# Keys mixed two rows at a time, and batch 0's plan of interleaved stages reordered

## Chip, cores and metric

One core of a Trainium2 chip. The metric is the device time of the whole kernel in microseconds (us). All runs quoted are fast; those of the kernel before run from 374.6 to 377.5 us over all sessions, so versions are compared by ratios within the same rounds. A ratio here is the mean time of one kernel's fast runs over that of the other's of the same rounds, so it is not quite the ratio of the medians that are quoted beside it.

## The reference

Attention within blocks whose keys and values are first mixed across blocks by a normalized 8x8 matrix `P` per head, then a mixture of four two-layer experts. Cut to what matters (`P` comes from five rounds of exponential and normalization of `sort_net`):

```python
B, H, S, D = 4, 8, 768, 64            # 8 blocks of 96 rows
k_sorted = einsum('bhij,bhjcd->bhicd', P, k_b)
v_sorted = einsum('bhij,bhjcd->bhicd', P, v_b)
attn = softmax(scale * q_b @ k_sorted.T)          # block by block
x = (attn @ v_sorted) as [3072, 512]
out = sum over e of p[:, e] * (relu(x @ w1[e]) @ w2[e])   # w1 [4,512,1024]
```

## The kernel before

TensorE runs the experts of batch b in three chunks of 256 rows; the attention of batch b+1 is cut into small stages which a plan puts into slots between groups of expert matmuls. `(1, 5, st_s, 1)` means: chunk 1, slot 5, scores of the second pair of heads. In batch 0 a chunk has slots 0 to 5 behind the groups of the first layer (16 matmuls each) and 6 to 12 behind the products of the second.

```python
    def load_queries(b, heads=range(H)):           # one load per head, on GpSimd
        ...
            nc.gpsimd.dma_start(t[:, h // 2, :, h % 2, :], q[b, h].rearrange("(t p) d -> p t d", p=P))

    def st_q(b, pr):                               # queries of a pair, transposed by a DMA from SP
        qT = att.tile([P, R, P], F16, name=f"qT_{b}_{pr}", tag="qT", bufs=3)
        nc.sync.dma_start_transpose(
            qT[:], natural[(b, "q")][:, pr].rearrange("p t h d -> p (t h d)")
        )
        ...

    def st_k(b, pr):                               # keys of a pair, mixed and transposed
        ps = psa([P, R, P], F32, f"ps_k_{b}_{pr}")
        for r in range(R):
            for hh in range(2):
                h = 2 * pr + hh
                nc.tensor.matmul(
                    ps[ds(D * hh, D), r, :],
                    head(b, "k", h)[:, r, :],
                    PIk[(b * H + h) // 4][:, h % 4, :, :].rearrange("p i c -> p (i c)"),
                    start=True, stop=True,
                )
        kT = kTs[pr % 2]
        nc.scalar.copy(
            kT[:, 0:S].rearrange("p (i r c) -> p i r c", i=NB, r=R),
            ps.rearrange("p r (i c) -> p i r c", c=CP),
        )

    def st_s(b, pr):                               # scores: 16 matmuls that read kT and qT
        kT, qT = kTs[pr % 2], qTs[(b, pr)]
        pss = [psa([P, 2, 512], F32, f"ps_s_{b}_{pr}_{hh}") for hh in range(2)]
        ...

    # st_n loads a pair's queries; st_lv, st_lk, st_lq load the next batch's values, keys, queries
    PLAN0 = [
        (0, 9, st_v, 0), (0, 10, st_q, 0), (0, 10, st_v, 1), (0, 11, st_k, 0), (0, 11, st_n, 1), (1, 0, st_q, 1),
        (1, 0, st_s, 0), (1, 0, st_n, 2), (1, 1, st_k, 1), (1, 1, st_v, 2), (1, 2, st_v, 3), (1, 3, st_a, 0),
        (1, 4, st_x, 0), (1, 3, st_q, 2), (1, 4, st_n, 3), (1, 5, st_s, 1), (1, 6, st_k, 2), (1, 8, st_a, 1),
        (1, 7, st_lv, 0), (1, 9, st_x, 1), (1, 10, st_s, 2), (1, 9, st_lv, 1), (1, 9, st_q, 3), (1, 11, st_k, 3),
        (1, 12, st_a, 2), (1, 12, st_lk, 0),
        (2, 0, st_lq, 0), (2, 1, st_x, 2), (2, 2, st_lk, 1), (2, 2, st_s, 3), (2, 8, st_a, 3), (2, 9, st_x, 3),
    ]

    def chunk(b, c, slot, done=()):                # [...] parts of batch 0's second layer
        def f1():
            nc.scalar.copy(p1[:], product("p1", blk(0, 0), "b11"))
            slot()
            gtt(oa1, oa1, p1[:], ALU.add)          # gtt: GpSimd, tt: VectorE
        ...
        def store(n, tile):
            nc.sync.dma_start(o[:, 2 * c + n, :], tile[:])
        ...
            next(sums0)                            # a weight difference on VectorE
            tt(u2[:], product("p6", sm(1), "t2"), p1[:], ALU.add)
            slot()
```

`psa` and `psm` are pools of two PSUM buffers each: `psa` for the stages, `psm` for the experts.

The softmax here doesn't subtract the row's maximum and nothing guards it: scores larger than these inputs give would overflow.

Of the kernel before, what the change touches and what calls it, by code (L numbers as in the profile page):

```python
# [9 lines left out]
F32 = mybir.dt.float32  # L10
# [7 lines left out]
def kernel(  # L18
# [11 lines left out]
    nc = tc.nc  # L30

    B, H, S, D = q.shape
# [33 lines left out]
    def psa(shape, dtype, name):  # L66
        state["n"] += 1
        return psA.tile(shape, dtype, tag="ps", name=name)
# [47 lines left out]
    def head(b, nm, h):  # L116
        return natural[(b, nm, h // 4)][:, h % 4, :, :]
# [117 lines left out]
    qTs = {}  # L235

    def warm(n):
        ps = psA.tile([P, 4, P], F32, tag="ps", name=f"ps_w_{state['n']}")
        state["n"] += 1
        for m in range(n):  # L240
            nc.tensor.matmul(ps[:, m % 4, :], dummy, dummy, start=True, stop=True)  # L241
# [21 lines left out]
    nc.gpsimd.tensor_copy(ident6, ident[0:R, 0:R])  # L263
    for it in range(5):
        nc.scalar.activation(sn[:], sn[:], AF.Exp, bias=0.0, scale=1.0)
        if it >= 3:
            h_q(it - 3, 0, nc.scalar.copy)
            warm(20 - 8 * (it - 3))
        nc.vector.tensor_reduce(srow[:], sn[:], AX.X, ALU.add)
        nc.vector.reciprocal(srow[:], srow[:])  # L270
        nc.vector.tensor_tensor(sn[:], sn[:], srow[:].broadcast_to([GH, NB, NB]), ALU.mult)
        nc.vector.tensor_reduce(scol[:], sn[:].rearrange("p i j -> p j i"), AX.X, ALU.add)
        nc.vector.reciprocal(scol[:], scol[:])
        if it < 4:
            nc.vector.tensor_tensor(
                sn[:], sn[:],
                scol[:].rearrange("p j o -> p o j").broadcast_to([GH, NB, NB]),
                ALU.mult,
            )
            if it:  # L280
                next(p_steps)
# [87 lines left out]
        qTs[(b, pr)] = qT.rearrange("p t x -> p (t x)").rearrange("p (i x) -> p i x", i=NB)  # L369

    def st_k(b, pr):
        ps = psa([P, R, P], F32, f"ps_k_{b}_{pr}")
        for r in range(R):
            for hh in range(2):
                h = 2 * pr + hh
                nc.tensor.matmul(  # L376
                    ps[ds(D * hh, D), r, :],
                    head(b, "k", h)[:, r, :],
                    PIk[(b * H + h) // 4][:, h % 4, :, :].rearrange("p i c -> p (i c)"),
                    start=True, stop=True,  # L380
                )
        kT = kTs[pr % 2]
        nc.scalar.copy(  # L383
            kT[:, 0:S].rearrange("p (i r c) -> p i r c", i=NB, r=R),
            ps.rearrange("p r (i c) -> p i r c", c=CP),
        )

    def st_s(b, pr):
        kT, qT = kTs[pr % 2], qTs[(b, pr)]
# [190 lines left out]
    def stage(b, f, pr):  # L580
# [18 lines left out]

    PLAN0 = [  # L600
        (0, 9, st_v, 0), (0, 10, st_q, 0), (0, 10, st_v, 1), (0, 11, st_k, 0), (0, 11, st_n, 1), (1, 0, st_q, 1),
        (1, 0, st_s, 0), (1, 0, st_n, 2), (1, 1, st_k, 1), (1, 1, st_v, 2), (1, 2, st_v, 3), (1, 3, st_a, 0),
        (1, 4, st_x, 0), (1, 3, st_q, 2), (1, 4, st_n, 3), (1, 5, st_s, 1), (1, 6, st_k, 2), (1, 8, st_a, 1),
        (1, 7, st_lv, 0), (1, 9, st_x, 1), (1, 10, st_s, 2), (1, 9, st_lv, 1), (1, 9, st_q, 3), (1, 11, st_k, 3),
        (1, 12, st_a, 2), (1, 12, st_lk, 0),
        (2, 0, st_lq, 0), (2, 1, st_x, 2), (2, 2, st_lk, 1), (2, 2, st_s, 3), (2, 8, st_a, 3), (2, 9, st_x, 3),
    ]


# [135 lines left out]
    def chunk(b, c, slot, done=()):  # L745

        es = range(E) if b else range(1, E)
        todo = [e for e in es if e not in done]
        chunk_first(b, c, todo, todo[0], slot)
        for w in range(1, 4 if b or c else 3):  # L750
            h_sums(E - 1, w)
        if (b, c) != (B - 1, R // 2 - 1):
            nxt = (b, c + 1) if c + 1 < R // 2 else (b + 1, 0)
            pbs[nxt] = load_p(*nxt)

        blk = lambda kh, tok: (lambda e, f: Hb[:, e, kh * KH + f, ds(tok * P, P)])
        sm = lambda n: (lambda e, f: Sb[:, n, e, ds(f * P, P)])

        def product(n, lhs, rhs):
            ps = psm([P, DH], F32, f"ps_{n}_{b}_{c}")  # L760
            for e in es:
                for f in range(KH):
                    nc.tensor.matmul(  # L763
                        ps[:], lhs(e, f), Ts[e][rhs][:, f, :],
                        start=(e == es[0] and f == 0), stop=(e == E - 1 and f == KH - 1),
                    )
            return ps[:]

        if b:
            oa, ob = [moeo.tile([P, Dm], F32, name=f"{n}_{b}_{c}", tag="oacc") for n in ("oa", "ob")]  # L770
        else:
            oa, ob = oaccs[2 * c], oaccs[2 * c + 1]
        p1, p5, u2, u3 = [moe.tile([P, DH], F32, name=f"{n}_{b}_{c}", tag=n, bufs=1) for n in ("p1", "p5", "u2", "u3")]
        tt, gtt = nc.vector.tensor_tensor, nc.gpsimd.tensor_tensor
        o = out[ds(b * S, S), :].rearrange("(t p) d -> p t d", p=P)
        oa1, oa2, ob1, ob2 = oa[:, 0:DH], oa[:, DH:Dm], ob[:, 0:DH], ob[:, DH:Dm]
        if b:
            nc.scalar.copy(p1[:], product("p1", blk(0, 0), "b11"))  # L778
            slot()
            nc.scalar.copy(ob1, product("p4", blk(1, 1), "n4"))  # L780
            slot()
            tt(oa1, product("p2", blk(1, 0), "b21"), p1[:], ALU.add)
            slot()
            nc.scalar.copy(p5[:], product("p5", sm(0), "t1"))
            slot()
            for e in es:
                h_sums(e, 4)
            tt(u2[:], product("p6", sm(1), "t2"), p1[:], ALU.add)  # L788
            slot()
            gtt(oa2, u2[:], p5[:], ALU.add)  # L790
            tt(u3[:], product("p7", sm(2), "t3"), u2[:], ALU.add)
            slot()
            gtt(ob2, u3[:], p5[:], ALU.add)
            tt(ob1, ob1, u3[:], ALU.add)
            nc.sync.dma_start(o[:, 2 * c + 1, :], ob[:])
            tt(oa2, product("p3", sm(3), "b22"), oa2, ALU.add)
            slot()
            nc.sync.dma_start(o[:, 2 * c, :], oa[:])
            return
        def f1():  # L800
            nc.scalar.copy(p1[:], product("p1", blk(0, 0), "b11"))
            slot()
            gtt(oa1, oa1, p1[:], ALU.add)

        def f2():
            tt(oa1, product("p2", blk(1, 0), "b21"), oa1, ALU.add)
            slot()

        def f3():
            tt(oa2, product("p3", sm(3), "b22"), oa2, ALU.add)  # L810
            slot()

        def f4():
            tt(ob1, product("p4", blk(1, 1), "n4"), ob1, ALU.add)
            slot()

        def f5():
            nc.scalar.copy(p5[:], product("p5", sm(0), "t1"))
            slot()
            gtt(oa2, oa2, p5[:], ALU.add)  # L820
            gtt(ob2, ob2, p5[:], ALU.add)

        def last(u3):
            gtt(ob2, u3, ob2, ALU.add)
            tt(ob1, ob1, u3, ALU.add)

        def store(n, tile):
            nc.sync.dma_start(o[:, 2 * c + n, :], tile[:])

        if c == 0:  # L830

            steps = weight_sums(E - 1, nc.vector)
            f1()
            for e in todo:
                h_sums(e, 4)
            next(steps)
            f2()
            next(steps)
            h_sums(E - 1, 3)
            f3()  # L840
            next(steps)
            f5()
            next(steps)
            tt(u3[:], product("p7", sm(2), "t3"), p1[:], ALU.add)
            slot()
            ps6 = product("p6", sm(1), "t2")
            tt(u2[:], ps6, p1[:], ALU.add)
            tt(u3[:], ps6, u3[:], ALU.add)
            slot()
            gtt(oa2, u2[:], oa2, ALU.add)  # L850
            store(0, oa)
            last(u3[:])
            f4()
            store(1, ob)
        else:
            f1()
            f4()
            f2()
            f5()
            for e in todo:  # L860
                h_sums(e, 4)
            next(sums0)
            tt(u2[:], product("p6", sm(1), "t2"), p1[:], ALU.add)  # L863
            slot()
            gtt(oa2, u2[:], oa2, ALU.add)
            next(sums0)
            tt(u3[:], product("p7", sm(2), "t3"), u2[:], ALU.add)
            slot()
            last(u3[:])
            store(1, ob)  # L870
            f3()
            store(0, oa)
# [75 lines left out]
    for qd in range(2):  # L948
# [8 lines left out]
        [(h_v, 1, 1, act)],  # L957
        [(h_s, 0, 2)],
        [(h_w, 0, vec), (h_s, 1, 2)],
        [(h_w, 1, vec), (h_a, 0, 2)],  # L960
        [(h_s, 0, 3), (h_a, 1, 2)],
        [(h_s, 1, 3), (h_a, 0, 3)],
        [(h_x, 2, act), (h_a, 1, 3)],
# [65 lines left out]
```

## Time and profile before

| | before |
|---|---|
| time | 375.25 us (374.92 to 375.5), over all sessions 374.62 to 377.49 |
| span in the profile | 373.0 us |
| TensorE, VectorE, ScalarE, GpSimd busy | 98%, 70%, 20%, 24% |
| granted TensorE clock | 0.999 |

The prediction below shows the lines on what bounds it.

`natq` are the queries as loaded and `qT` their transposes. The weights, on the same GpSimd queue (POOLq) as the queries, need 27 us to land (median): they are issued faster than they land, and the last of them, issued at about 22 us, lands at about 60.

### The profile page before, as it was taken

The numbers are of one execution on the slowest core, as the hardware profiler recorded it, in microseconds if no ns is written. First come the engines' busy times: TensorE is split into PE (matmuls) and PEld (weight loads), VectorE is DVE, ScalarE is ACT, GpSimd is POOL, SyncE is SP. The second block draws the span as 40 slices with busy tenths as digits, with TensorE's granted clock in tenths as the row PEclk, the third lists the DMA queues.
The fourth block names the chain that finished last, engine by engine and source line by source line (L and its number), as shares of the span: only waits on it lengthen the run. The fifth ranks groups of instructions, "written<-read, shape, count | busy, mean of one in ns | idle before, by whom it ended". The sixth has DMA issues, their size and how long they took to land.

```text
span 373.0 us, 9188 instructions
## 1 busy us (share of the span) xinstructions
PE 366.3 (98%) x4013; PEld 314.9 (84%) x4013; DVE 261.2 (70%) x470; ACT 73.9 (20%) x120; POOL 87.9 (24%) x122
## 2 busy tenths in 40 slices
PE   8999999999999999999999999999999999999996
PEld 8785858888888888888898888888889888888885
DVE  5654798679888774795694684696695693774872
ACT  2673330423210233012100224012101000000000
POOL 8772101804577203002911000000000001001001
PEclk9999999999999999999999999999999999999999
DMA  7999999999995658642962322505203101121001
GB/s 104 207 207 229 208 209 197 190 163 143 187 154 137 110 77 133 126 80 43 124 71 48 101 66 60 138 2 77 79 2 79 57 15 44 56 47 50 19 3 56
DMA packets 69603, 38.25 MB, mean 103 GB/s; under 512 B 40374, under 2 KB 64444, under 8 KB 69564
## 3 DMA queue, kind: packets, MB, share of 16 engines
q0 software_dynamic: 34640, 17.83, 37.6%
q1 hardware_dynamic: 34924, 19.85, 26.0%
q8 instruction: 31, 0.51, 0.6%
q14 instruction: 8, 0.07, 0.1%
HBM read 42.00 MB, written 6.34 MB: 130 GB/s over the span
## 4 chain that ended last, share of the span: by engine, by line
PE 87%; DMA 8%; DVE 2%; POOL 1%; issue 1%; ACT 0%; DVEq 0%
PE ps_h L730 40%; PE ps_p L763 35%; DMA w<-in_moe_w_dram 4%; PE ps_o L670 3%; DMA qT<-natq 2%; PE ps_w L241 2%; DMA natq<-in_q_dram 2%; PE ps_h L635 1%; PE ps_s L393 1%; PE ps_a L425 1%; PE ps_k L376 1%; PE ps_v L345 1%; POOL sn L284 0%; DVE xsl L410 0%; POOL T L136 0%
## 5 line engine op out<-in xcount | busy, mean ns | idle before, releaser
L730 PE MATMUL ps_h<-xT,w 128*128 128x256 f16 x1440 | 163.0, 273 | 0.0
L730 PEld LDWEIGHTS <-w 128*128 128x128 f16 x1440 | 139.5, 98 | 17.8
L736 DVE SCALAR_TENSOR_TENSOR Hb<-ps_h,pb 128x1024 f16<-128x1024 f32 x90 | 110.1, 1224 | 40.1 <-PE ps_h L730 38.3
L763 PEld LDWEIGHTS <-Sb 128*128 128x128 f16 x720 | 69.5, 98 | 9.6 <-issue 0.5
L763 PEld LDWEIGHTS <-Hb 128*128 128x128 f16 x540 | 52.1, 98 | 6.8 <-issue 0.4
L790 POOL TENSOR_TENSOR oa<-u,p 128x256 f32<-128x256 f32 x9 | 6.5, 723 | 176.7 <-issue 161.9
L763 PE MATMUL ps_p<-w,Sb 128*128 128x256 f16 x360 | 43.2, 273 | 0.3 <-DVE u L863 0.3
L763 PE MATMUL ps_p<-w,Hb 128*128 128x256 f16 x360 | 43.2, 273 | 0.0
L763 PE MATMUL ps_p<-T,Sb 128*128 128x256 f16 x360 | 42.3, 273 | 0.0
L400 ACT ACTIVATE ET<-ps_s 96x768 f16<-96x768 f32 x24 | 18.1, 802 | 54.4 <-PE ps_s L393 54.4
L114 POOL DMA_DIRECT2D natq<-in_q_dram x24 | 19.9, 851 | 14.3 <-DMA w<-in_moe_w_dram 10.2
L778 ACT COPY p<-ps_p 128x256 f32<-128x256 f32 x9 | 3.4, 373 | 93.3 <-PE ps_p L763 50.1
L763 PE MATMUL ps_p<-T,Hb 128*128 128x256 f16 x180 | 21.6, 273 | 0.0
L715 DVE TENSOR_TENSOR Sb<-Sb,Hb 128x512 f16<-128x512 f16 x45 | 19.6, 436 | 0.4
L717 DVE TENSOR_TENSOR Sb<-Hb 128x512 f16<-128x512 f16 x45 | 18.8, 418 | 0.0
L713 DVE TENSOR_TENSOR Sb<-Hb 128x512 f16<-128x512 f16 x45 | 18.8, 417 | 0.0
L410 DVE TENSOR_TENSOR xsl<-ps_a,rz 96x512 f16<-96x512 f32 x24 | 16.5, 686 | 0.8
L719 DVE TENSOR_TENSOR Sb<-Hb,Sb 128x512 f16<-128x512 f16 x45 | 16.6, 427 | 0.0
L383 ACT CAST kT<-ps_k 128x768 f16<-128x768 f32 x12 | 9.6, 799 | 35.4 <-PE ps_k L376 35.3
L788 DVE TENSOR_TENSOR u<-ps_p,p 128x256 f32<-128x256 f32 x9 | 3.8, 426 | 17.9 <-PE ps_p L763 17.9
L351 ACT CAST vo<-ps_v 128x768 f16<-128x768 f32 x12 | 9.5, 801 | 21.5 <-PE ps_v L345 19.8
L103 POOL DMA_DIRECT2D nat_k<-in_k_dram x8 | 6.1, 767 | 31.9 <-PE ps_k L376 27.8
(131 smaller groups left out, 300.9 us busy)
## 6 DMA issues: line engine op xcount, KB each, us to landing
w<-in_moe_w_dram POOLq DMA_DIRECT2D x7, 1024.0 KB, 27.1
pb<-p_dram SPq DMA_DIRECT2D x12, 512.0 KB, 5.1
nat_k<-in_k_dram POOLq DMA_DIRECT2D x8, 384.0 KB, 7.4
nat_v<-in_v_dram POOLq DMA_DIRECT2D x8, 384.0 KB, 8.6
vs<-vo SPq DMA_DIRECT2D x36, 66.0 KB, 4.6
natq<-in_q_dram POOLq DMA_DIRECT2D x24, 96.0 KB, 4.5
out_dram<-ob SPq DMA_DIRECT2D x9, 256.0 KB, 2.3
out_dram<-oa SPq DMA_DIRECT2D x9, 256.0 KB, 2.3
```

The source lines that it names most:

```text
L114: nc.gpsimd.dma_start(t[:, h // 2, :, h % 2, :], q[b, h].rearrange("(t p) d -> p t d", p=P))
L383: nc.scalar.copy(kT[:, 0:S].rearrange("p (i r c) -> p i r c", i=NB, r=R), ps.rearrange("p r (i c) -> p i r c", c=CP),)
L400: nc.scalar.activation(ETs[2 * (pr % 2) + hh][:, 0:S].rearrange("c (a x) -> c a x", a=2), pss[hh][0:BLK, :, 0:HS], AF.Exp, bias=0.0, scale ...
L410: nc.vector.tensor_tensor(xsl[:, :, hh, :].rearrange("c (a i) d -> c a i d", a=2), av[:, :, :, 0:D], rz[:].broadcast_to([BLK, 2, HB, D]), ...
L670: nc.tensor.matmul(ps, h0(fc)[:, ds(t * P, P)], w2sb[0][:, fc, :], start=(fc == 0), stop=(fc == NFC - 1),)
L713: tt(sm[0], blk(0, 1), blk(1, 1), ALU.add)
L715: tt(sm[1], sm[0], blk(0, 0), ALU.subtract)
L717: tt(sm[2], blk(0, 0), blk(0, 1), ALU.subtract)
L719: tt(sm[3], blk(1, 0), sm[1], ALU.subtract)
L730: nc.tensor.matmul(ps[:, f, :], w1sb[e][:, kc, ds((4 * g + f) * P, P)], xT[:, kc, ds(2 * c * P, 2 * P)], start=(kc == 0), stop=(kc == NKC ...
L736: nc.vector.scalar_tensor_tensor(out=Hb[:, e, ds(4 * g, 4), :], in0=ps[:], scalar=0.0, op0=ALU.max, in1=pb[:, ds(e, 1), :].broadcast_to([P ...
L763: nc.tensor.matmul(ps[:], lhs(e, f), Ts[e][rhs][:, f, :], start=(e == es[0] and f == 0), stop=(e == E - 1 and f == KH - 1),)
```

## The change

Its intent: fewer and fuller matmuls for the keys; value mixing of batch 1 behind the second pair's scores; loads of batch 2 at other slots; fewer waits on VectorE in batch 0; a shorter last store. The diff, cut to its core:

```diff
-        ps = psA.tile([P, 4, P], F32, tag="ps", name=f"ps_w_{state['n']}")       # warm()
+        ps = psM.tile([P, 4, P], F32, tag="ps", name=f"ps_w_{state['n']}")
@@ five rounds of the start
-        if it >= 3:
-            h_q(it - 3, 0, nc.scalar.copy)
-            warm(20 - 8 * (it - 3))
+        if it == 4:
+            for qd in range(2):
+                h_q(qd, 0, nc.scalar.copy)
+            warm(30)
@@ st_k
+        ps = psa([P, 2, 512], F32, f"ps_k_{b}_{pr}")
+        pk = ps[:, :, 0:R // 2 * P].rearrange("p h (a x) -> p h a x", x=P)
+        for hh in range(2):
+            h = 2 * pr + hh
+            for a in range(R // 2):
                 nc.tensor.matmul(
-                    ps[ds(D * hh, D), r, :],
-                    head(b, "k", h)[:, r, :],
+                    pk[:, hh, a, :],
+                    head(b, "k", h)[:, ds(2 * a, 2), :].rearrange("p r d -> p (r d)"),
                     ...
+        kT = kTs[pr % 2][:, 0:S].rearrange("p (i a r c) -> p r a i c", a=R // 2, r=2, c=CP)
+        for hh in range(2):
+            for r in range(2):
+                nc.scalar.copy(
+                    kT[ds(D * hh, D), r],
+                    pk[ds(D * r, D), hh].rearrange("p a (i c) -> p a i c", c=CP),
+                )
@@ PLAN0
-        (1, 0, st_s, 0), (1, 0, st_n, 2), (1, 1, st_k, 1), (1, 1, st_v, 2), (1, 2, st_v, 3), (1, 3, st_a, 0),
-        (1, 4, st_x, 0), (1, 3, st_q, 2), (1, 4, st_n, 3), (1, 5, st_s, 1), (1, 6, st_k, 2), (1, 8, st_a, 1),
-        (1, 7, st_lv, 0), (1, 9, st_x, 1), (1, 10, st_s, 2), (1, 9, st_lv, 1), (1, 9, st_q, 3), (1, 11, st_k, 3),
-        (1, 12, st_a, 2), (1, 12, st_lk, 0),
-        (2, 0, st_lq, 0), (2, 1, st_x, 2), (2, 2, st_lk, 1), (2, 2, st_s, 3), (2, 8, st_a, 3), (2, 9, st_x, 3),
+        (1, 0, st_s, 0), (1, 0, st_n, 2), (1, 1, st_k, 1), (1, 2, st_lv, 0), (1, 3, st_s, 1),
+        (1, 3, st_q, 2), (1, 4, st_k, 2), (1, 4, st_n, 3), (1, 5, st_v, 2), (1, 6, st_v, 3), (1, 6, st_lk, 0),
+        (1, 7, st_a, 0), (1, 8, st_x, 0), (1, 9, st_a, 1), (1, 9, st_q, 3), (1, 9, st_lv, 1),
+        (1, 10, st_x, 1), (1, 11, st_s, 2), (1, 12, st_lq, 0),
+        (2, 0, st_a, 2), (2, 1, st_k, 3), (2, 2, st_x, 2), (2, 2, st_lk, 1), (2, 3, st_s, 3),
+        (2, 8, st_a, 3), (2, 9, st_x, 3),
@@ last chunk of the last batch: the store of oa in two halves, the first behind product p2
+                nc.sync.dma_start(o[:, 2 * c, 0:DH], oa1)
+                nc.sync.dma_start(o[:, 2 * c, DH:Dm], oa2)
@@ f1
-            nc.scalar.copy(p1[:], product("p1", blk(0, 0), "b11"))
+            nc.scalar.copy(p1[:], product("p1", blk(0, 0), "b11", psa))
@@ chunks 1 and 2 of batch 0
+            tt(u2[:], product("p6", sm(1), "t2"), p1[:], ALU.add)
+            slot()
             next(sums0)
-            tt(u2[:], product("p6", sm(1), "t2"), p1[:], ALU.add)
-            slot()
             ...                                    # the second weight difference likewise behind u3
@@ values of batch 0
-        [(h_w, 1, vec), (h_a, 0, 2)],
+        [(h_w, 1, act), (h_a, 0, 2)],
```

More of the change, by code (lines that the diff above doesn't have):

```diff
@@ L371, in st_k @@
     def st_k(b, pr):
-        ps = psa([P, R, P], F32, f"ps_k_{b}_{pr}")
-        for r in range(R):
-            for hh in range(2):
-                h = 2 * pr + hh
+        ps = psa([P, 2, 512], F32, f"ps_k_{b}_{pr}")
[3 more added lines that the diff above has]
+            for a in range(R // 2):
                 nc.tensor.matmul(
-                    ps[ds(D * hh, D), r, :],
-                    head(b, "k", h)[:, r, :],
+                    pk[:, hh, a, :],
+                    head(b, "k", h)[:, ds(2 * a, 2), :].rearrange("p r d -> p (r d)"),
                     PIk[(b * H + h) // 4][:, h % 4, :, :].rearrange("p i c -> p (i c)"),
@@ L381, in st_k @@
                 )
-        kT = kTs[pr % 2]
-        nc.scalar.copy(
-            kT[:, 0:S].rearrange("p (i r c) -> p i r c", i=NB, r=R),
-            ps.rearrange("p r (i c) -> p i r c", c=CP),
-        )
+        kT = kTs[pr % 2][:, 0:S].rearrange("p (i a r c) -> p r a i c", a=R // 2, r=2, c=CP)
[5 more added lines that the diff above has]
+                )
     def st_s(b, pr):
@@ L757, in chunk, with product @@
         sm = lambda n: (lambda e, f: Sb[:, n, e, ds(f * P, P)])
-        def product(n, lhs, rhs):
-            ps = psm([P, DH], F32, f"ps_{n}_{b}_{c}")
+        def product(n, lhs, rhs, pool=psm):
+            ps = pool([P, DH], F32, f"ps_{n}_{b}_{c}")
             for e in es:
@@ L783, in chunk @@
             slot()
+            parts = 2 if (b, c) == (B - 1, R // 2 - 1) else 1
+            if parts == 2:
+                nc.sync.dma_start(o[:, 2 * c, 0:DH], oa1)
             nc.scalar.copy(p5[:], product("p5", sm(0), "t1"))
@@ L797, in chunk @@
             slot()
-            nc.sync.dma_start(o[:, 2 * c, :], oa[:])
+            if parts == 2:
+                nc.sync.dma_start(o[:, 2 * c, DH:Dm], oa2)
+            else:
+                nc.sync.dma_start(o[:, 2 * c, :], oa[:])
             return
         def f1():
-            nc.scalar.copy(p1[:], product("p1", blk(0, 0), "b11"))
+            nc.scalar.copy(p1[:], product("p1", blk(0, 0), "b11", psa))
             slot()
@@ L861, in chunk @@
                 h_sums(e, 4)
-            next(sums0)
             tt(u2[:], product("p6", sm(1), "t2"), p1[:], ALU.add)
             slot()
+            next(sums0)
             gtt(oa2, u2[:], oa2, ALU.add)
-            next(sums0)
             tt(u3[:], product("p7", sm(2), "t3"), u2[:], ALU.add)
@@ L869, in chunk @@
             last(u3[:])
+            next(sums0)
             store(1, ob)
```

## The prediction

> **What bounds the kernel now.** I read the page's first two parts, then TensorE's waits, then the chain that ended last piece by piece, then the DMA issues with their landing times in windows.
>
> ```profile
> PE 366.3 (98%) x4013; PEld 314.9 (84%) x4013; DVE 261.2 (70%) x470; ACT 73.9 (20%) x120; POOL 87.9 (24%) x122
> PE   8999999999999999999999999999999999999996
> DMA  7999999999995658642962322505203101121001
> ```
>
> TensorE is busy from end to end at full clock (0.999), so the time is the sum of its work plus a few waits. ACT at 20% can take more work; DVE (70%) can only where it is not crowded. DMA is full for the first third.
>
> ```profile
> PE ps_R L296 <- DVE sn L284: 0.5, 1, 0.5
> PE ps_s L393 <- DMA qT<-natq: 0.3, 1, 0.3
> PE ps_p L763 <- DVE u L863: 0.3, 1, 0.3
> PE ps_a L534 <- DVE xsl L546: 0.2, 1, 0.2
> PE ps_o L670 <- DMA w<-in_moe_w_dram: 0.2, 1, 0.2
> ```
>
> All named waits of TensorE, with 1.1 us at the very start, make 2.6 us. So no change of waits alone can give 2%; only less matmul time can add to it. The chain shows what a stage costs (start, duration, piece):
>
> ```profile
> 121.57 0.33 PE ps_v L345 x2
> 121.90 1.75 PE ps_h L730 x16
> 123.64 0.33 PE ps_v L345 x2
> 123.97 1.75 PE ps_h L730 x16
> 125.72 0.46 PE ps_k L376 x12
> 126.17 5.35 PE ps_h L730 x48
> 131.52 0.45 PE ps_s L393 x16
> 131.97 1.85 PE ps_h L730 x16
> ```
>
> Sixteen 256-column matmuls take 1.75 us, 0.109 each. After the value mixing (full 128x128 array) the next block is undelayed; after the key mixing (64-wide outputs) 48 matmuls take 5.35 instead of 3 x 1.75 = 5.24, and 16 after the scores (64-deep) take 1.85. A stage that uses half of the array costs 0.10 us more behind it. That is true at each such place that I looked at.
>
> [...] In this trace eight transposes of N=128, each with its own weights, take 0.45 us (L489), so 56 ns each; I use 56. [...] 799 ns for 768 columns and 373 for 256 give 0.832; 384 columns take 477. [...] a query transpose behind two 256 KB stores took 7.9 us; in quiet stretches it takes 2.8.
>
> **The change part by part.** *Keys.* Twelve mixing stages go from 12 matmuls of 64-column weights to 6 of 128. By row L376 of the chain a stage is 0.456 us; after: 6 x 0.056 = 0.335. The 0.10 behind it should go too. (0.12 + 0.10) x 12 = **-2.7 us**. In return ACT does four copies of 64x384 (4 x 0.48 = 1.9 us) for one of 0.80, in all 12 x 1.1 = 13 us more, on an engine with 80% free. Latency: the scores that read the keys come two slots or more later (two are 2 x 1.75 = 3.5 us), against 2.1 us with the hop; so beside, not on, the path. The PSUM buffer is held 1.1 us longer. I walked the two buffers in order: the tightest place is the new first product in that pool behind the third keys of batch 1 (needed 4.2 us after the scores, freed at about 4.2), worth 0 to 0.1 us.
>
> *Batch 0's DVE order.* In the third chunk the first product ends at 107.62 + 12 x 0.109 = 108.93 and the next starts at 109.10, when L736 frees its buffer; and the third-last two end at 113.51 + 24 x 0.109 = 116.13 while the last starts at 116.61, behind L863, which stood behind a 1.22 us weight difference. A product in the other pool and the add ahead of the difference take both away: 0.17 + 0.48 = **-0.65**.
>
> *Values of batch 0 copied on ACT.* DVE's 0.69 us copy at 36.01 stands ahead of the normalization for which TensorE waits at 37.59: **-0.2**.
>
> *Last store in halves.* DVE ends at 369.81, the span at 373.0: 3.2 us for the store and the end. The last transfer shrinks from 256 to 128 KB; 256 KB land in 2.3 us when quiet[...], and the other row block's store, issued 0.6 us before, stays whole: **-0.3**.
>
> *Start.* The fifth exponential starts at 9.98, behind a 0.80 us query copy, though DVE was ready at 9.40: 0.5 us gained there. But TensorE then waits at 28.46 for a weight load that comes through a full DMA (about 205 GB/s in every window from 10 us on), so the gain becomes a wait there: **0**.
>
> *Plan of batch 1's stages.* This is where it can lose. The second pair's scores move from slot 5 of the second chunk to slot 3, with two value mixings (0.65) and one attention (0.48) put behind them. So TensorE reaches them 2 x 1.75 + 1.13, with 0.5 saved before, some 5 us earlier: at 78.8 instead of 84.0. What they need is the second query transpose:
>
> ```profile
> 69.25 7.02 DMA natq<-in_q_dram
> 76.27 0.02 issue
> 76.29 7.88 DMA qT<-natq
> 84.17 0.14 issue
> 84.30 0.52 PE ps_s L393 x16
> ```
>
> Its load is still issued in slot 11 of the first chunk, and the transpose still stands in SP's ring behind the two stores issued at 72.96, which land at about 80 and 82. So before was already on the edge (0.32 us of wait), and the change moves the reader but not the data. The six small stores of values issued at 79.9, during the transpose, move away, but a 384 KB load of batch 2 comes in between. If the transpose takes 5 to 6.5 us instead of 7.9, it lands at 81 to 82.5 and TensorE waits 2.2 to 3.7. I take **+3.0** in place of the 0.32 of before, so **+2.7** net. A wait here is not won back, since nothing after it has slack in TensorE's queue. The first pair's scores arrive 0.4 us earlier at a transpose that lands at 72.5: perhaps +0.1.
>
> Sum: -2.7 - 0.65 - 0.2 - 0.3 + 0 + 2.7 + 0.2 (the two small waits) = -0.95 us, which gives 374.3. I choose 373.8, half a microsecond lower, since two of the terms (the transpose with less traffic, the stores' tail) have more room below than above.
>
> **The rivals.** *A: no new wait.* With the value stores gone the transpose lands by 79 (2.8 us, as in the quiet stretches). For: those stores shared SP's ring and the 16 engines. Against: they came behind it in the ring, and the two 256 KB stores are ahead of it. Then 375.25 - 3.85 - 0.3 = 371.1. *B: the wait in full.* The transpose takes the 7.9 us of before or more, because batch 2's load takes its place; wait 5 to 5.5, time 376 to 377. For: the same ring order. Against: the load is in another ring. *C: weight loads set the pace of the keys.* [...] Against: the 56 ns of L489. *D: ACT's four copies hold TensorE up* in the later batches: eight stages of up to 0.3 us, 2.4 on top of 373.8, would be 376. Against: the buffer walk above.
>
> **Range and chances.** A gives the low end and B the high one; C or D on top of a middle wait lands between. Low 370.6, high 377.0. Two per cent are 7.5 us: faster would need twice the sum of all gains, slower a wait of 11 us. 0.01 and 0.02; 0.97 for the same.
>
> **What would show it.** Right: the key row falls to about 0.33 us a stage with six matmuls, and the block behind it to multiples of 1.75; ACT rises from 73.9 to about 87 us; L863 and the L736 edge vanish from TensorE's waits; TensorE waits for qT near 79 us for 2 to 4 us; the wait for weights at 28 us grows to about 0.7. Wrong: no wait for qT (A), a wait over 5 us (B), keys above 0.45 (C), or waits on ACT's kT copies in the batches after (D). A load of batch 2 that comes later than its reader would be something that I did not foresee.

The 0.335 us of a key stage is six times the 56 ns of L489; the -0.3 of the last store is the author's estimate. The 2.1 us for the four copies with the hop was measured later as 2.17 (from the end of the key matmuls at 75.05 us to that of the copies at 77.22, in the changed kernel). What the texts call SP's ring or another ring are the DMA queues SPq and POOLq of the profile; what they say of the ring's order rests on the 7.9 us beside the 2.8 alone, and e3 and e10 test it.

## More of the kernel before

One more view matters later: the list of DMA transfers, with the issuing queue, count, size and the median time from issue to landing in us.

```profile
w<-in_moe_w_dram POOLq DMA_DIRECT2D x7, 1024.0 KB, 27.1
nat_v<-in_v_dram POOLq DMA_DIRECT2D x8, 384.0 KB, 8.6
natq<-in_q_dram POOLq DMA_DIRECT2D x24, 96.0 KB, 4.5
out_dram<-oacc SPq DMA_DIRECT2D x6, 256.0 KB, 5.4
qT<-natq SPq DMA_TRANSPOSE x12, 4.9
```

## The result, and the profile after

The changed kernel took 379.38 us (378.95 to 381.26, six runs) against 375.18 for the kernel before in the same rounds: ratio 1.0118 (1.0093 to 1.0142). It is slower by over 1%, and above the range of the prediction.

The first two parts of its page, where the slices say where to look:

```profile
PE 364.4 (96%) x3939; PEld 316.0 (84%) x3939; DVE 261.0 (69%) x469; ACT 87.9 (23%) x157; POOL 86.8 (23%) x122
PE   8799999939999999999999999999999999999996
PEclk9999999997999999999999999999999999999999
DMA  8999999993999386934393221514204101111101
```

In the ninth slice (75 to 85 us) TensorE is busy for a third only; in the tenth its granted clock is 0.7. The waits of TensorE (line, what it waited for, total, times, longest):

```profile
PE ps_s L398 <- DMA qT<-natq: 6.1, 1, 6.1
PE ps_R L297 <- DVE sn L285: 1.3, 1, 1.3
PE ps_w L241 <- DVE Hb L141: 1.1, 1, 1.1
PE ps_mv L467 <- DMA nat_v<-in_v_dram: 0.4, 1, 0.4
PE ps_h L641 <- DMA w<-in_moe_w_dram: 0.4, 1, 0.4
```

The wait on L863 is gone, as meant, and the one for `qT` has grown from 0.3 to 6.1 us. The chain that ended last, around it:

```profile
68.86 7.13 DMA natq<-in_q_dram
75.99 0.02 issue
76.01 8.76 DMA qT<-natq
84.76 0.04 issue
84.81 0.82 PE ps_s L398 x16
85.63 3.53 PE ps_h L736 x16
89.16 0.64 PE ps_k L379 x6
89.80 2.17 PE ps_h L736 x16
91.96 0.33 PE ps_v L346 x2
```

The transpose lands at 84.8, 0.6 us later than before, while TensorE had been ready since 75.05 + 2 x 1.75 = 78.55. The second thing to see is behind it: the same 16 score matmuls take 0.82 us in place of 0.45, 16 expert matmuls 3.53 in place of 1.75, a key stage 0.64 in place of 0.33. TensorE runs at half speed. The view by windows has it in its column of the granted clock, the third from the end (window, then busy time and instructions of TensorE, its weight loads, DVE, ACT and POOL; then clock; DMA share and GB/s, which are not used here):

```profile
78.60:84.80 6.20, 0.10 (x1) 0.09 (x1) 1.89 (x3) 0.00 (x0) 0.00 (x0) 0.91 1.62 170
84.80:88.00 3.20, 3.19 (x28) 2.38 (x28) 0.00 (x0) 1.50 (x2) 0.00 (x0) 0.50 0.96 156
88.00:92.00 4.00, 4.00 (x30) 3.25 (x29) 1.56 (x3) 1.89 (x4) 0.00 (x0) 0.68 0.01 1
92.00:96.00 4.00, 4.00 (x49) 3.49 (x48) 3.93 (x9) 1.88 (x3) 1.46 (x2) 1.00 0.36 72
```

The keys, in batch 1, beside the lines that the prediction showed of before:

```profile
130.79 1.75 PE ps_h L736 x16
132.54 0.33 PE ps_k L379 x6
132.87 5.24 PE ps_h L736 x48
138.11 0.45 PE ps_s L398 x16
138.56 1.85 PE ps_h L736 x16
```

A stage takes 0.33 in place of 0.46 and the block behind it 5.24 in place of 5.35. So the span is best read in stretches whose ends the timelines give (us; the last column is an experiment told below):

| stretch | before | after | run e8 |
|---|---|---|---|
| start to batch 0's first product | 60.44 | 60.05 | 61.76 |
| to the second pair's scores of batch 1 | 23.86 | 24.76 | 18.40 |
| to batch 1's first layer | 33.62 | 39.93 | 37.42 |
| to VectorE's last addition | 251.47 | 249.66 | 249.66 |
| to the end | 3.61 | 3.3 | 3.3 |

The second and third stretch hold the same stages before and after together (in the kernel after, its four key stages are the shorter ones), but 5 us of the work were moved across the scores. Together they grew by 7.2 us; the fourth, which has eight key stages and nothing else that changed, shrank by 1.81 (8 x 0.226), and the end by 0.3.

### The profile page after: what moved, and what is told of

Same layout as the page of the kernel before. It is cut to its first block, busy times and chain, and to the rows that moved or that the text cites. A ratio compares the mean times of both kernels' runs of the same rounds, so it can differ in the third digit from the quotient of the medians.

```text
span 377.7 us, 9075 instructions
## 1 busy us (share of the span) xinstructions
PE 364.4 (96%) x3939; PEld 316.0 (84%) x3939; DVE 261.0 (69%) x469; ACT 87.9 (23%) x157; POOL 86.8 (23%) x122
## 4 chain that ended last, share of the span: by engine, by line
PE 88%; DMA 8%; POOL 2%; issue 1%; DVE 0%; ACT 0%; DVEq 0%; ACTq 0%; POOLq 0%
PE ps_h L736 40%; PE ps_p L769 35%; DMA w<-in_moe_w_dram 3%; PE ps_h L641 3%; PE ps_o L676 3%; DMA qT<-natq 2%; DMA natq<-in_q_dram 2%; PE ps_a L430 2%; PE ps_s L398 1%; PE ps_k L379 1%; PE ps_v L346 1%; POOL nat_k L103 0%; PE ps_s L522 0%; POOL nat_v L103 0%; PE ps_a L539 0%
## 5 line engine op out<-in xcount | busy, mean ns | idle before, releaser
L736 PE MATMUL ps_h<-xT,w 128*128 128x256 f16 x1440 | 165.5, 275 | 0.0
L388 ACT CAST kT<-ps_k 64x384 f16<-64x384 f32 x48 | 22.7, 473 | 39.1 <-PE ps_k L379 38.2
L114 POOL DMA_DIRECT2D natq<-in_q_dram x24 | 19.9, 853 | 11.7 <-DMA w<-in_moe_w_dram 9.9
```

The source lines that it names most:

```text
L388: nc.scalar.copy(kT[ds(D * hh, D), r], pk[ds(D * r, D), hh].rearrange("p a (i c) -> p a i c", c=CP),)
L736: nc.tensor.matmul(ps[:, f, :], w1sb[e][:, kc, ds((4 * g + f) * P, P)], xT[:, kc, ds(2 * c * P, 2 * P)], start=(kc == 0), stop=(kc == NKC ...
```

## The experiments

The theory at this point: the reader was moved 5 us ahead of data that did not move, and the 6 us of idle time that this makes put TensorE at half clock for some time more; everything else in the change gains. The rivals: another part (four copies on ScalarE) shares in the loss; the clock fell for another reason; and for what holds the transpose, either the two stores ahead of it in SP's queue (A) or the loads of GpSimd's queue beside it (B).

### e1: the plan put back

```diff
-    PLAN0 of the change
+    PLAN0 of before          # all else as changed
```

> The changed kernel with the plan of batch 0's stages put back. Theory (the plan alone costs: a 6.1 us wait for the query transpose and some 2.9 us of work at half clock behind it, while the other parts save about 4.2 us): no wait for qT over 0.6 us, granted clock 0.999 and 371 us. Rival (another part of the change, such as the four ACT copies, shares in the loss): still above 373.

Measured: 373.0 us (before: 374.96), ratio 0.9930 (0.9898 to 0.9962), clock 1.000. The plan makes the loss: without it the change gains. But it gains 0.7%, not 1.1%, and the waits of TensorE say why:

```profile
PE ps_p L768 <- ACT ET L405: 0.9, 1, 0.9
PE ps_a L430 <- ACT kT L388: 0.6, 1, 0.6
...
PE ps_s L398 <- DMA qT<-natq: 0.2, 1, 0.2
```

With the old plan the first product, now in the stages' pool, comes right behind the scores and waits for their exponential; and the attention waits 0.6 us for a buffer behind the four key copies. So the expected 371 was missed, and the rival is right to 1.5 us under the old plan. The new plan has value mixing between the scores and the product, and the changed kernel has neither wait.

### e6 and e5: plan alone, keys alone, on the kernel before

```diff
 e6: before
-    PLAN0 of before
+    PLAN0 of the change
 e5: before
-    st_k of before
+    st_k of the change
```

> The kernel before with the new plan of batch 0's stages alone. Theory (the plan by itself makes the wait and the slow clock): wait for qT 5 to 6 us, half clock for some 5 us behind it, time 375.0 + 5.5 + 2.5 = 383. Rival (the wait needs the earlier arrival that the other parts bring): wait under 3 us, no slow clock, 376 to 378.

> The kernel before with the new key mixing alone. Prediction: 0.335 us a stage in place of 0.456 and no 0.10 us behind it, 2.7 us less in all, 372.4. Rival (ACT's four copies keep a PSUM buffer or the keys too long where batch 0's plan puts value mixing and attention right behind them, as the 0.6 us wait on the key copies in the run with the old plan suggests): 0.5 to 1.5 us of it are lost to a wait on kT or vo in batch 0, 373 to 374.

Measured, with before at 376.17 in these rounds: e6 382.07 us, ratio 1.0168 (1.0136 to 1.0199), a wait for `qT` of 5.0 us and the scores at 0.82 us; e5 373.14 us, ratio 0.9926 (0.9896 to 0.9955). The plan alone is enough for wait and slow clock. The keys give 0.74%, 2.8 us, with an interval from 1.7 to 3.9. The profile of e5 shows less, a span of 371.5 for 373.0: 1.8 us are gained behind batch 0, and nothing in batch 0, where four shorter stages should give 0.9. One wait on their copies took 0.6 of that, as the rival had it:

```profile
PE ps_a L429 <- ACT kT L387: 0.6, 1, 0.6
```

### e12: the rest alone

```diff
-    PLAN0 and st_k of the change
+    PLAN0 and st_k of before          # all else as changed
```

> The kernel before with all of the change but the plan and the key mixing: the order of batch 0's additions, the first product in the other pool, values copied on ACT, the start, and the halved last store. Prediction: 0.65 + 0.2 + 0.3 = 1.2 us less, 374. From the run with the old plan, where the first product in the pool of the scores waited 0.9 us for their exponential: 0.3 us less, 374.7 to 375.2.

Measured: 375.71 us (374.54 to 377.03) against 376.51, ratio 0.9992 (0.9933 to 1.0051): nothing that the noise would show. Its waits hold `PE ps_p L764 <- ACT ET L401` with 0.9 us, the same as e1. In its profile the end is 0.3 us shorter, as meant, but the two middle stretches together take 57.39 us for 57.48 before, so the 0.65 of the additions' order is lost at that one wait, and the start is 0.4 longer. The changed kernel, with the new plan, has no such wait.

### e8: the query early

```diff
-        (0, 9, st_v, 0), (0, 10, st_q, 0), (0, 10, st_v, 1), (0, 11, st_k, 0), (0, 11, st_n, 1), (1, 0, st_q, 1),
+        (0, 9, st_v, 0), (0, 10, st_q, 0), (0, 10, st_q, 1), (0, 10, st_v, 1), (0, 11, st_k, 0),
-            load_queries(1, range(2))
+            load_queries(1, range(4))             # at the start, behind the weights
```

> The changed kernel with the query load of batch 1's second pair issued at the start behind the first pair's, and its transpose issued right behind the first pair's, so that the data are there before the scores. Theory (the lateness of this one transpose costs 9 us of the changed kernel): it lands by 76, no wait for qT at the second pair's scores, granted clock 0.999, time 370.5 to 371.5. Rival (the time goes elsewhere once it is taken away, such as to the next transpose, or to DVE, which the wait let catch up): over 373.

Measured: 372.13 us (371.93 to 372.57) against 376.17, ratio 0.9901 (0.9866 to 0.9936). No wait on `qT` is left, and the rest of the plan is kept:

```profile
76.57 3.66 PE L736 MATMUL ps_h<-xT,w 128*128 128x256 f16 x32
80.16 0.51 PE L398 MATMUL ps_s<-qT,kT 64*128 64x96 f16 x16
80.60 1.92 PE L736 MATMUL ps_h<-xT,w 128*128 128x256 f16 x16
```

The time is 0.6 us above the range expected, and far from the rival's. So this one transpose costs the changed kernel 379.38 - 372.13 = 7.25 us between medians, and the ratios say 2.2%, some 8 us. In the stretches above it costs 6.4 us in the second and 2.5 in the third, 8.9 in all; the profile of e8 gives 1.7 back at its start. It ran at half clock from about 14 to 21 us, which led to e13.

### e2 and e11: dummy matmuls in the wait

```diff
         pss = [psa([P, 2, 512], F32, f"ps_s_{b}_{pr}_{hh}") for hh in range(2)]
+        if (b, pr) == (1, 1):
+            for _ in range(105):                  # e11: 60
+                nc.tensor.matmul(pss[0][:, 0, 0:P], ident[:], ident[:], start=True, stop=True)
```

> The changed kernel with 105 matmuls of the identity put into the first PSUM buffer of the second pair's scores of batch 1, ahead of the real ones, so that TensorE is busy while it waits for the query transpose (105 x 0.056 = 5.9 us in a wait of 6.1 to 6.3). Theory (the idle time itself makes the clock fall): the scores take 0.45 us in place of 0.82 and the blocks after them 1.75 in place of 3.5, the granted clock is 0.999, and the time falls by 2.9 us from 379.4 to 376.5. Rival (the clock falls for another reason[...]): the slow stretch stays and the time is 379 to 380.

> As the run with 105 identity matmuls in the wait, but with 60 (3.4 us), so that they end before the transpose lands and some 2.8 us of idle time are left. Theory (idle time of 4 to 6 us brings the clock down, and 105 were sometimes too many): granted clock 1.000 or nearly, no stretch at half clock behind the scores, and 376 to 377, no more than 378.5. Rival (2.8 us of idle time are enough, or the clock has another cause): scores at 0.82 us and blocks at 3.5, 378 to 380.

Measured: e2 378.48 us (376.98 to 380.12), ratio 1.0081 (1.0040 to 1.0123), granted clock 1.000 in all four runs; e11 378.09 us (377.14 to 379.4), ratio 1.0050 (0.9994 to 1.0105), clock 0.995 to 1.000. The timeline of e11:

```profile
79.60 3.51 PE L398 MATMUL ps_s<-ident 128*128 128x128 f16 x60
85.69 0.52 PE L401 MATMUL ps_s<-qT,kT 64*128 64x96 f16 x16 [2.58 <-DMA qT<-natq]
86.14 1.92 PE L739 MATMUL ps_h<-xT,w 128*128 128x256 f16 x16
87.90 0.50 PE L379 MATMUL ps_k<-PIk,nat_k 128*128 128x128 f16 x6
```

The transpose comes no earlier, yet the work behind it is at full speed. From the scores to batch 1's first layer it takes 37.43 us in e2 and 37.56 in e11, as in e8 (37.42), in place of 39.93: the half clock costs 2.4 to 2.5 us, and idle time of TensorE is its cause. In time, the ratios of e2 and e11 are 0.4 and 0.7% below that of the changed kernel, 1.4 to 2.6 us. The intervals overlap, so the trace shows this, and the times only agree with it. Neither run reached the time expected of it (376.5; 376 to 377). For e2 this fits a transpose that lands at another time from run to run while 105 dummies always take 6 us; no trace of those other runs was read. Two of e11's four runs have a mean clock of 0.995. The profile of e14 has that too, with 3.4 us at half clock (below), so an estimate for each of the two is the same; no trace shows where.

How long an idle time it takes, over the profiles (idle: from the end of the last block to the scores; time at half clock: for each window twice what its mean clock lacks of 1, times its length, since windows of 0.25 us in the changed kernel show 1.00 or 0.50 and other values only at the two edges, 0.90 and 0.95; for e6 and e10, without windows, twice what the scores and the blocks behind them took over their usual length, which leaves out what fell within the wait):

| run | idle us | at half clock us |
|---|---|---|
| e10 | 1.3 | 0 |
| e11 | 2.7 | 0 |
| e4 | 4.3 | 6.8 |
| e3 | 4.7 | 3.4 |
| e6 | 5.2 | 3.5 or more |
| e14 | 5.4 | 3.4 |
| changed kernel | 6.3 | 6.9 |
| e10, third pair's scores | 9.8 | 4.2 or more |

Where windows were taken, the times at half clock are near 3.4 us or near twice that. The runs give no sharp limit of idle time: the clock falls 5.2 us after the last block in the changed kernel (at 83.7 us). From the mean clocks of longer windows an estimate is 2.7 in e4 (0.82 from 79.3 to 83.6 us), 5.0 in e3 and 5.4 in e14 (0.56 and 0.51 in the windows from the scores on), while e11 passed 2.7 us at full clock (1.00 from 83.1 to 85.7). At the start two profiles with some 2 us of idle time differ as well: e8 fell to half clock (0.50 to 0.51 from 14 to 20 us) 2.3 us after work had resumed at 11.7, and e14 did not (1.00 in every window from 8 to 22). What else decides it was not shown.

### e3, e4, e10, e14: what holds the transpose

```diff
 e3: the two stores of batch 0's first chunk are issued in slot 4 of chunk 1, behind the scores
 e4: PLAN0
-        (1, 2, st_lv, 0), ... (1, 6, st_lk, 0)
+        (1, 7, st_lv, 0), ... (1, 12, st_lk, 0)
 e10: PLAN0
-        (1, 0, st_n, 2), (1, 2, st_lv, 0), (1, 3, st_q, 2), (1, 4, st_n, 3), (1, 6, st_lk, 0)
+        (1, 7, st_n, 2), (1, 7, st_q, 2), (1, 7, st_n, 3), (1, 7, st_lv, 0), (1, 8, st_lk, 0)
 e14: load_queries(1, range(4)) at the start as in e8, st_q of the second pair left at (1, 0)
```

> The changed kernel with the two 256 KB stores of batch 0's first row blocks issued behind the second pair's scores, so that the query transpose no longer stands behind them in SP's ring. Theory A (the stores ahead of it in the ring hold the transpose): it takes 4 to 5 us instead of 8.8, the wait falls to 2 us or less, the clock stays up, time 372 to 373. Theory B (the loads of the other queue share the engines and set its pace): the transpose still takes 7 us or more, the wait stays over 4 us and the clock falls, time 377 or more.

> The changed kernel with batch 2's first value load and first key load put back to slots 7 and 12 of the second chunk, so that neither is in flight beside the query transpose. Theory A (the stores ahead in SP's ring set the pace): transpose 8 us or so, wait 5 to 6 us, clock still falls, 378 to 379.4. Theory B (the moved loads lengthen it): transpose 5 to 6 us, wait about 3, time 373 to 376.

> The changed kernel with all loads that GpSimd issues between 71 and 76 us (queries of the third and fourth pair, values and keys of batch 2) and the third pair's transpose put behind the first product of the second chunk, so that nothing of the loads' queue is in flight beside the second pair's transpose; the two stores stay ahead of it in SP's ring. Theory B of before (the loads set its pace): it takes 3 to 5 us, the wait is 0 to 2.5 us, the clock stays at full, time 372 to 374 unless the third pair's own transpose is now late. Theory A (ring order): 7 us or more and a wait over 4 us.

> The changed kernel with the second pair's query load issued at the start, its transpose left in its place behind the two stores. It can then start at about 73.7 in place of 76. If a transpose among those loads takes 7 to 8.5 us whenever it starts, it lands at 81 to 82 and TensorE waits 2.3 to 3.3 us: 373.5 to 376, clock up or barely down. If the load was what it really waited for, and the engines are freer at 73: no wait, 372.

| run | time us | ratio | transpose issued | takes | lands |
|---|---|---|---|---|---|
| before | 375.2 | 1 | 76.3 | 7.9 | 84.2 |
| changed kernel | 379.4 | 1.0118 | 76.0 | 8.8 | 84.8 |
| e3 stores behind it | 379.7 | 1.0106 | 76.5 | 8.5 | 85.0 |
| e4 loads of batch 2 back | 378.1 | 1.0073 | 76.5 | 7.1 | 83.6 |
| e10 loads all behind it | 384.8 | 1.0245 | 77.2 | 3.9 | 81.1 |
| e14 its load early | 379.5 | 1.0089 | 74.9 | 10.7 | 85.6 |

The loads beside the transpose in the changed kernel, and the transpose there and in e10 (us from issue to landing):

```profile
nat_v<-in_v_dram POOLq DMA_DIRECT2D x1, 384.0 KB, 10.5
natq<-in_q_dram POOLq DMA_DIRECT2D x2, 96.0 KB, 11.3
nat_k<-in_k_dram POOLq DMA_DIRECT2D x1, 384.0 KB, 12.9
qT<-natq SPq DMA_TRANSPOSE x1, 8.8
```

```profile
qT<-natq SPq DMA_TRANSPOSE x1, 3.9
```

Theory A falls as the main cause: with the stores still ahead but nothing of GpSimd's queue in flight (e10) the transpose takes 3.9 us, and with the stores out of its way (e3) it still takes 8.5. (In e3 the loads went out 2 us later, with the whole start, so that more of them were beside it; a small share of the stores is not excluded.) Theory B holds. Without the two loads of batch 2 (e4) it takes 1.7 less; with those loads it takes 8.4 to 8.8 in four profiles (changed kernel, e2, e6, e11), so 1.7 is outside that spread. But e4's time of 378.1 and its wait of 4.1 miss what B expected of it (373 to 376, about 3), for the queries of two pairs are still beside it. e10 also moved the third pair's transpose away; that one does not make the difference, since before the change it was issued only at 83.8 and the second still took 7.9. In the kernel before, four query transposes from 180 to 240 us take 2.8 (median; 2.7 at 205.4 us, with no load of GpSimd's queue in flight), against 3.9 behind the two stores and 7.1 to 10.7 beside loads here.

Started earlier into the same loads (e14) the transpose takes 10.7 and lands at 85.6, no sooner than when it was issued at 76.0. So both of e14's expectations were wrong (its 379.5 includes 1.5 us of wait for the first pair's transpose as well). The early load that e8 also has is not enough; the transpose too has to go out before that crowd. It does not outlast the whole crowd: the last queries and the keys of batch 2 land after it, at about 86 to 89 us in the changed kernel. What in those loads sets its pace, their bytes or their packets (from 75 to 77 us 1109 of 1292 are under 512 B), was not tested.

Why the loads are there at all is seen in the timeline of GpSimd, before and after:

```profile
71.44 3.33 POOL L114 DMA_DIRECT2D natq<-in_q_dram  x4
```

```profile
71.06 1.69 POOL L114 DMA_DIRECT2D natq<-in_q_dram  x2
72.72 0.78 POOL L103 DMA_DIRECT2D nat_v<-in_v_dram  x1
73.48 1.67 POOL L114 DMA_DIRECT2D natq<-in_q_dram  x2
75.51 0.76 POOL L103 DMA_DIRECT2D nat_k<-in_k_dram  x1 [0.36 <-PE ps_k L379]
```

The plan puts these four into slots 0, 2, 4 and 6, which TensorE reaches between 72 and 93 us. GpSimd did not wait for them: its timeline has one wait among the four, of 0.36 us on key matmuls. So they went out from 71.06 to 76.3 us, ahead of the scores in slot 3. They are spread over batch 0 in the text, but not on the chip. In e10 the loads stand behind an addition that waits for a product (15.58 us), and there they do come late, from 88.91 us on. Then the third pair's queries are late in turn: a wait of 9.6 us and half clock again, hence 384.8.

### e13: more warming at the start

```diff
-            warm(30)
+            warm(50)                              # on top of e8
```

> The run with query load and transpose moved early, with 50 warming matmuls in place of 30 at the start, since TensorE idled 1.9 us there and then ran at half clock from 13.7 to 20.5 in its profile. If that stretch costs time to the end: 371 in place of 372.1. If the full DMA (weights at 28 us) hides it: 372 again, with the clock at 1.000 in all runs.

Measured: 372.37 us (371.85 to 372.81) against 376.51, ratio 0.9893 (0.9854 to 0.9932), clock 0.999 to 1.000. The stretch at half clock is gone and the time is that of e8. Batch 0's first product started at 61.60, as in e8 (61.76). So the slow stretch at the start was hidden, as the second expectation says; e8's own runs agree, with 372.28 us at a clock of 0.991 and 371.93 to 372.57 at 1.000. Why both runs reach this point 1.2 to 1.3 us later than the kernel before is not settled: over all profiles that time lies between 60.05 and 62.1, also for kernels with the same start.

e8 and e13 are the best versions found: 1.0 to 1.1% faster than the kernel before and 2.2% faster than the change.

## Why the prediction was wrong

**What bounds it, and the keys: right.** "0.12 + 0.10" a stage was measured as 0.226 (1.81 over eight stages), and a stage in batch 0 of the changed kernel takes 0.34 as well (74.71 to 75.05). That the keys alone gave 2.8 us (1.7 to 3.9) for 2.7 is in part luck, since e5's profile shows only 1.5. The 56 ns of L489 held: six matmuls in 0.33 us. Why the first block on the full array loses 0.10 us behind matmuls on half of it (forms 64*128 and 128*64; 1.85 in place of 1.75 behind the scores, 5.35 in place of 5.24 behind the old key stage) was not tested. ScalarE went to 87.9 us for the 87 expected.

**VectorE's order, half store: right in the changed kernel** (both edges gone; end 3.61 to 3.3, the last store 128 KB in 1.8 us in place of 256 KB in 2.1), but not parts by themselves, since the pool of the first product costs 0.9 us without the new plan (e1, e12). The 0.2 us wait for the normalization (L534) is gone from the changed kernel's list, as the copies on ScalarE were to do; no run has them alone.

**The plan: the step that failed is the term "+3.0", and one term is missing.** The prediction found the place, the wait and the reason ("the change moves the reader but not the data"). It then wrote: "If the transpose takes 5 to 6.5 us instead of 7.9, it lands at 81 to 82.5 and TensorE waits 2.2 to 3.7." It took 8.8, and TensorE waited 6.1. The argument was that six small stores go away and the load of batch 2 "is in another ring", and that the two stores ahead set the pace. The runs show the reverse: the other queue's loads set it (e10: 3.9 us without them), the stores ahead were not the main cause (e3), and the change put two more loads there (e4: 1.7 us). Rival B had this and was given as the high end, but with "5 to 5.5".

**The missing term: what a long wait does behind itself.** Rival B was priced at 376 to 377 by the wait alone. The stretch behind it cost 2.5 us more at half clock (e2, e11). With 6.1 in place of 3.0, and 2.5 on top, the sum of the prediction comes to 374.3 + 3.1 + 2.5 = 379.9, near the 379.4 measured.

**The start:** predicted as worth nothing, and within the spread of the profiles it is; the wait for weights at 28 us did not grow to 0.7 in the changed kernel's profile, but showed as 0.4 at 19 us.

## What to carry to other kernels

When a stage is pulled forward, follow each of its operands back to the issue of its transfer and move that too; what counts is being ahead of a crowd of loads: here a start 1.1 us earlier within it gained nothing (e14), while a transpose that went out before it ended the wait (e8). A slot in a plan need not time a load: here those of slots 0 to 6, which TensorE reached between 72 and 93 us, went out from 71.06 to 76.3 us, since none waited for over 0.36 us, while behind an addition that waited they came at 88.91 (e10). And price a long wait of TensorE with the half clock that follows: all six waits of over 4 us here brought it, and in the changed kernel 6 us of waiting cost 8.9 in the profiles.
